# Tiled matmuls in pairs, another order of the first loads, and transposes planned to land later, in an attention and MoE kernel

## The chip, the core and the metric

The kernel runs on one core of one Trainium2 chip. The metric is the device time of one execution in microseconds. Engines are named as in the profile: PE is TensorE (PEld its weight loads), ACT is ScalarE, DVE is VectorE, POOL is GpSimd, SP is SyncE. POOL and SP issue the DMAs here. A time given as "22.5" without more is a moment, counted from the start of the profiled span.

## What is computed

Eight batches of 8 heads, 576 positions and 64 dimensions go through two softmax attentions, and the result through two dense layers with a smooth cut in between:

```python
def sm_attn(qq, kk, vv):
    s = scale * np.matmul(qq, kk.transpose(0, 1, 3, 2))
    a = np.exp(s - np.max(s, axis=-1, keepdims=True))
    a = a / (np.sum(a, axis=-1, keepdims=True) + 1e-09)
    return np.matmul(a, vv)
p_packed = sm_attn(p, k, v)          # p: 32 packed queries per head
out = sm_attn(q, p_packed, p_packed)
x = out.transpose(0, 2, 1, 3).reshape(4608, 512)
h = x @ w_in                         # 512 x 2048
g = np.where(h >= 1, h, np.where(h <= -1, 0.0, (h + 1) ** 2 / 4))
y = g @ w_out                        # 2048 x 512
```

All inputs and the output are float32; the kernel loads with a cast and multiplies in bfloat16.

## The kernel before, in words

The kernel never forms the attention's output. For each batch it works in these steps, whose names are those of the planner's tasks and of the tiles in the profile:

- **kT, qT**: k and q are turned so that the head dimension lies on partitions. For batches 0 to 2 PE does it (`trans`: tile `tp`, L365, then a copy on ACT or DVE); from batch 3 on (`TURNED = 3`) SP issues DMA transposes (`turned`, L489).
- **sc** (L386, tile `sp`): scores of the packed queries against k, then the exponential on ACT (`ex`).
- **pk** (L404, L410): the packed values from `ex` and v, with the sums (`rs`); copies and an addition make `ppT`.
- **s2** (L436, tile `s`): scores of q against the packed values, for one half of the heads (two halves g); ACT takes the exponential (`eT`), PE sums it over 32 rows (`sm`, L446), ACT takes logarithm and exponential (`ln`, `rc`), DVE makes the normalised weights `A`.
- **M** (L478, tile `mp`): packed values times one quarter of w_in, four quarters per batch; a copy on ACT or DVE puts the result into `M`.
- **h** (`hidden_tile`, L521): `M` times `A`, 16 tiles of 128 hidden features per batch, four matmuls each. ACT and DVE apply the smooth cut (`x`, L526 to L533) and write `hT` (L536).
- **o** (`out_tile`, L571): `hT` times w_out. Two batches form a pair of 1152 tokens, that is nine output tiles of 128 rows with 16 matmuls each (one for each of the 16 row blocks of w_out). `ob` is the copy out, and SP issues the writes (L577).

The s2 and M matmuls have 64 rows and 32 columns, so eight of them lie beside each other in PE's array; all others use 128 columns. A task carries the tiling as its `mode`.

The order of the instructions is fixed when the kernel is built. The class `Plan` holds a task for each step with its costs (`C`), dependencies and buffers, simulates the engines DMA, SP, ACT, DVE and PE, and emits each task in the order in which it came up. Three wide PSUM buffers (`"W"`, `NW = 3`) go round among all steps but o, which has two of its own (`"O"`). The DMA engine of the plan takes the loads strictly one after the other, in the order in which they are added; on the chip POOL issues them in that order. `land` is what the plan adds from the end of a load's own cost to its landing, `xt` and `xland` are the same two for a DMA transpose, `p` is when the first part of p is there. While PE has nothing to do in the plan and fewer than three output tiles have begun, it gets dummy matmuls on zeros (L634), which begin at `wake`.

The loads before (L293 to L300) stand in this order: k, v, q of batch 0; w_in and w_out by quarters in turn; k, q, v of batch 1; the rest of p; then k, q, v of batches 2 to 7 as their buffers come free (two buffers for each).

Of the kernel before, what the change touches and what calls it, by code (L numbers as in the profile page):

```python
# [8 lines left out]

C = dict(load=3.0, first=3.8, w_in=2.65, w_out=2.55, out=9.0, p=3.1, land=1.9, xt=5.0, xland=2.5,
         tpp=0.06, tp=0.042, sc=0.034, pk=1.05, s2=0.25, sm=0.245, M=0.345, h=0.49, o=0.217, switch=0.05,
         pTc=0.1, Tca=1.12, Tcd=0.76, ex=0.82, ppT=0.42, ppo=0.41, ppa=0.4, ppd=0.2, rs=0.18, eT=0.74, ln=0.65, rc=0.68, A=0.82,
         Mca=1.0, Mcd=1.22, x=0.65, ta=0.683, td=0.457, hT=0.758, oba=0.585, obd=0.69,
         array=0.2, wake=2.0, tell=0.04, feed=0.1, slack=0.6, margin=0.15, wait=0.5)
NW, NO, NX, NB = 3, 2, 5, 6
DW = 256
TURNED = 3
# [2 lines left out]
class Task:  # L22

    def __init__(self, engines, cost, key, deps, fn, takes, readers, frees, mode, slack, after, holds):
        self.engines, self.cost, self.key, self.deps, self.fn = engines, cost, key, list(deps), fn
        self.takes, self.readers, self.frees, self.mode = takes, readers, frees, mode
        self.slack, self.after, self.holds = slack, after, holds
        self.users, self.end, self.slot, self.gone = [], None, None, 0.0


class Plan:
# [24 lines left out]
    def ready(self, t, e):  # L56
        at = 0.0
        for d in t.deps:
            if e == "PE":
                lag = 0.0 if d.on == "PE" else C["feed"] + (C["margin"] if t.slack is None else t.slack)  # L60
            else:
                lag = C["array"] if d.on == "PE" else C["tell"] if d.on != e else 0.0
            at = max(at, d.end + lag)
        if t.takes:
            room = self.rooms[t.takes][self.count[t.takes] % len(self.rooms[t.takes])]
            if room is None:
                return None
            at = max(at, room + (C["feed"] if e == "PE" else 0.0))
        return at

    def choose(self, e, given, waiting):
# [37 lines left out]
    def run(self, idle):  # L109
        self.line = [t.seq for t in self.tasks if t.engines == ("DMA",)]  # L110
        left = {}
        given = {e: [] for e in self.ENGINES}
        for t in self.tasks:
            left[t] = len(t.deps)
            for d in t.deps:
                d.users.append(t)
            if not t.deps:
                for e in t.engines:
                    given[e].append(t)
        n = len(self.tasks)  # L120
        while n:
            best = None
            for e in self.ENGINES:
                c = self.choose(e, given, n)
                if c is not None and (best is None or c[0] < best[0]):
                    best = c[0], e, c[1]
            if self.count["O"] < 3:
                c, step = self.choose("PE", given, n), DW / 2400
                self.now["PE"] = max(self.now["PE"], C["wake"])
                if (c is None or c[0] > self.now["PE"] + step) and best is not None and best[0] > self.now["PE"]:  # L130
                    idle()
                    self.now["PE"] += step
# [12 lines left out]
            self.log.append((at, at + cost, e, t))  # L145
            if t.takes:
                room = self.rooms[t.takes]
                t.slot = self.count[t.takes] % len(room)
                room[t.slot] = None
                self.count[t.takes] += 1  # L150
                if t.readers == 0:
                    room[t.slot] = t.end + t.holds
            if t.frees is not None:
                f = t.frees
                f.gone = max(f.gone, t.end)
                f.readers -= 1
                if f.readers == 0:
                    self.rooms[f.takes][f.slot] = f.gone
            if len(t.engines) > 1:
                t.fn(e)  # L160
            elif e in ("ACT", "DVE"):
                t.fn(e)
            else:
                t.fn()
            for x in t.engines:
                given[x].remove(t)
            for u in t.users:
                left[u] -= 1
                if left[u] == 0:
                    for x in u.engines:  # L170
                        given[x].append(u)
            n -= 1
# [3 lines left out]
def kernel(  # L176
# [10 lines left out]
    nc = tc.nc  # L187
# [16 lines left out]
    G = 2  # L204
# [8 lines left out]
    NF = d_ff // FW  # L213
# [15 lines left out]
    PE, ACT, DVE, DMA, SP = "PE", "ACT", "DVE", "DMA", "SP"  # L229
# [42 lines left out]
    def add_load(nm, b, parts=1, deps=(), cost="load"):  # L272
        for i, hs in enumerate([ALL] if parts == 1 else HS):
            L[nm, b, i] = add(DMA, C[cost] / parts, -1, deps, lambda nm=nm, b=b, hs=hs: load(nm, b, hs))
        if parts == 1:
            L[nm, b, 1] = L[nm, b, 0]
# [15 lines left out]
    L["v", 0, 0] = L["v", 0, 1] = add(DMA, C["first"], -1, (), lambda: None)  # L292
    add_load("q", 0, 2, cost="first")  # L293
    for f in range(NF):
        add_weights("in", f)
        add_weights("out", f)
    add_load("k", 1)
    add_load("q", 1)
    add_load("v", 1)
    L["p"] = add(DMA, C["load"] / 6, -1, (), lambda: nc.gpsimd.dma_start(p_nat[:, PB * 2:], p_v[:, PB * 2:]))  # L300


    def both(fns, cost_a, cost_d, key, deps, **kw):
# [42 lines left out]
    def attention(b, key):  # L346
# [28 lines left out]
        def scores(i, deps):  # L375
            box, ky = {}, key["sc" + str(i)]

            def mm():
                sp = wide([P, 1024], f32, "sp")
                box["sp"] = sp[:TP, :E * X * Q * NP].rearrange("p (e y) -> p e y", e=E)  # L380
                for e in range(E):
                    o = sp[:, e * X * Q * NP:(e + 1) * X * Q * NP].rearrange("p (x a n) -> p x a n", x=X, a=Q)
                    for a in range(Q):
                        h = head(i, a)
                        w = (h % 4 * E + e) * TP
                        nc.tensor.matmul(o[:, :, a], kT()[:, i, w:w + P], pT[:, b, h], start=True, stop=True)  # L386

            def ev(eng):
                nc.scalar.activation(ex()[:, :, i].rearrange("p e x a n -> p e (x a n)"), box["sp"], AF.Exp, scale=scale)  # L389
            t = add(PE, C["sc"] * 12, ky, deps, mm, takes="W", readers=1, mode=0)  # L390
            return t, add(ACT, C["ex"], ky, [t] + old("pk"), ev, frees=t)

        def packed(deps):
            box, ky = {}, key["pk"]

            def mm():
# [11 lines left out]
                for g in range(G):  # L408
                    for c in range(NC):
                        nc.tensor.matmul(s_[:, g], ex_[:, c // X, g, c % X].rearrange("p a n -> p (a n)"), ones2[:TP],  # L410
                                         start=(c == 0), stop=(c == NC - 1))
            t = add(PE, C["pk"], ky, [L["v", b, 0]] + deps, mm, takes="W", readers=3, mode=0)
            war = old("s2", "M")

            def odd(eng):
# [12 lines left out]
        def weights(g, deps, r):  # L428
# [27 lines left out]
            def norm(eng):  # L456
                nc.vector.scalar_tensor_tensor(A()[:, g], box["eT"], rs()[:, g, :1], box["rc"], ALU.mult, ALU.mult)  # L457
            p_ = K.get((b - 1, "A" + str(g)), [])
            t = add(PE, C["s2"], ky, deps, mm, takes="W", readers=1, mode=2)
            e_ = add(ACT, C["eT"], ky, [t, r] + p_, exp2, frees=t)  # L460
            t2 = add(PE, C["sm"], km, [e_], mm2, takes="W", readers=1, mode=0)
            l_ = add(ACT, C["ln"], km, [t2] + last.get("ln", []), ln, frees=t2)
            i_ = add(ACT, C["rc"], km, [l_] + p_, inv)
            a_ = add(DVE, C["A"], km, [i_] + K.get((b - 2, "h"), []), norm)
            last["ln"] = [i_]
            K[b, "A" + str(g)] = [a_]
            return t, e_, a_

        def mk(f, deps):
            box, ky = {}, key["M" + str(f)]  # L470

            def mm():
                mp = box["mp"] = wide([P, G, FW], f32, "mp")
                for a in range(Q):
                    for g in range(G):
# [1 line left out]
                        y = h % 2  # L477
                        nc.tensor.matmul(mp[a * NP:(a + 1) * NP, g], pp_of(y, h),  # L478
                                         w_in_sb[y * D:(y + 1) * D, h // 2, f * FW:(f + 1) * FW], start=True, stop=True)
            t = add(PE, C["M"], ky, deps + [L["in", f]], mm, takes="W", readers=1, mode=2)  # L480
            cp = lambda eng: copy(M()[:, :, f * FW:(f + 1) * FW], box["mp"])(eng)
            war = K.get((b - 2, "h"), [])
            if (b, f) == (0, 0):
                return t, add(DVE, C["Mcd"], ky, [t], cp, frees=t)
            return t, both(cp, C["Mca"], C["Mcd"], ky, [t] + war, frees=t)

        def turned(nm, i, dst, prev):
            def go():
# [176 lines left out]
```

## Time and profile before

| | |
|---|---|
| median of 3 runs | 257.83 us (256.91 to 258.0) |
| the profiled execution | 256.86 us |
| its span | 255.1 us |
| PE busy in the span | 244.8 us (96%) |
| ACT, DVE busy | 183.9 us, 176.0 us |
| dummy matmuls on PE | 135, 18.3 us |
| loads on POOL's queue | 18.55 MB |

The busy time of PE counts matmuls from start to end, and successive matmuls overlap, so a difference of two starts tells what a group holds of PE better than its duration does. Rows of a timeline give the start, the stretch, the engine, line and operation, out<-in with shapes, the count of instructions merged into the row, and in brackets the idle time before it with what ended it. A row of the waits gives engine, tile and line, what ended the wait, then the sum, the number of times and the longest, in us. A row of DMA issues gives the queue, the size, and the time from the issue to landing.

### The profile page before, as it was taken

To read this page: it belongs to the slowest core of one execution; us is meant where nothing else is said; L and a number is where in the kernel's file an instruction comes from. 1 tells how busy PE (TensorE), PEld (TensorE's weight loads), DVE (VectorE), ACT (ScalarE), POOL (GpSimd) and SP (SyncE) were. 2 spreads that over 40 slices of the span, in tenths; PEclk is the share of its full clock that TensorE was granted. 3 is DMA by queue.
4 is the path that set the end of the run, shared out by engine and by line. 5 is a ranking of instruction groups with operands and counts; after the bars stand their busy time and mean duration, and the time that the engine had idled before them with its cause. 6 is when DMAs were issued, how large, how long until landed. Compare 5 with 4: busy or idle time off the path is not lost.

```text
span 255.1 us, 5583 instructions
## 1 busy us (share of the span) xinstructions
PE 244.8 (96%) x2254; PEld 146.4 (57%) x2287; DVE 176.0 (69%) x303; ACT 183.9 (72%) x295; POOL 28.6 (11%) x41
## 2 busy tenths in 40 slices
PE   7999999899999999999999999999999999999993
PEld 5977557367547555744664556555654465644452
DVE  5236998788899987998847885878366887940000
ACT  3236987888999988989949896989668896841110
POOL 8533312112001300210101000000000000000000
PEclk9999999999999999999999999999999999999998
DMA  7999999999999999999999940211021111132223
GB/s 104 189 207 206 207 204 194 240 210 212 179 200 177 205 182 214 185 193 180 188 150 174 234 116 14 71 44 42 5 80 41 45 41 41 44 82 82 57 70 84
DMA packets 54778, 34.38 MB, mean 135 GB/s; under 512 B 27488, under 2 KB 50272, under 8 KB 54752
## 3 DMA queue, kind: packets, MB, share of 16 engines
q0 software_dynamic: 24624, 18.55, 48.9%
q1 hardware_dynamic: 29968, 15.34, 32.5%
q8 instruction: 18, 0.29, 0.4%
q10 hardware_dynamic: 160, 0.13, 0.2%
q14 instruction: 8, 0.07, 0.1%
HBM read 37.22 MB, written 9.44 MB: 183 GB/s over the span
## 4 chain that ended last, share of the span: by engine, by line
PE 73%; DMA 14%; ACT 3%; DVE 3%; issue 2%; POOL 2%; ACTq 0%; POOLq 0%
PE o L571 42%; PE h L521 22%; DMA p_nat<-in_p_dram 8%; DMA w_out_sb<-in_moe_w_out_dram 7%; PE mp L478 3%; PE sp L386 2%; DVE hT L536 2%; ACT x L526 1%; PE sm L446 1%; PE s L436 1%; ACT x L533 1%; PE tp L365 1%; PE pk L404 1%; POOL w_in_sb L280 1%; POOL q L254 1%
## 5 line engine op out<-in xcount | busy, mean ns | idle before, releaser
L571 PE MATMUL o<-w_out_sb,hT 128*128 128x512 bf16 (+1 forms) x559 | 138.5, 373 | 2.4 <-issue 1.0
L536 DVE SCALAR_TENSOR_TENSOR hT<-x 128x576 bf16<-128x576 f32 x128 | 93.7, 755 | 18.0 <-PE o L571 12.7
L526 ACT ACTIVATE x<-h 128x576 f32<-128x576 f32 x128 | 79.1, 658 | 10.3 <-PE h L521 8.2
L571 PEld LDWEIGHTS <-hT 128*128 128x128 bf16 x592 | 55.9, 98 | 52.4 <-issue 4.8
L521 PE MATMUL h<-A,M 128*128 128x288 bf16 x512 | 79.2, 286 | 1.0 <-ACT M L308 0.3
L521 PEld LDWEIGHTS <-M 128*128 128x128 bf16 x512 | 48.8, 98 | 25.9 <-issue 1.9
L531 DVE TENSOR_SCALAR x<-x 128x576 f32<-128x576 f32 x93 | 42.0, 460 | 16.0 <-ACT x L526 15.4
L308 ACT COPY ob<-o 128x512 f32<-128x512 f32 (+1 forms) x27 | 15.5, 574 | 35.1 <-PE o L571 34.9
L308 ACT CAST M<-mp 128x1024 bf16<-128x1024 f32 x24 | 24.2, 1015 | 0.3 <-PE mp L478 0.3
L308 DVE COPY ob<-o 128x512 f32<-128x512 f32 (+1 forms) x10 | 6.6, 662 | 25.4 <-PE o L571 25.1
L533 ACT ACTIVATE x<-x 128x576 f32<-128x576 f32 x35 | 23.5, 684 | 0.5
L634 PE MATMUL o<-zeros 128*128 128x256 bf16 x135 | 18.3, 286 | 1.2 <-DVE zeros L242 1.2
L389 ACT ACTIVATE ex<-sp 96x768 bf16<-96x768 f32 x16 | 12.9, 804 | 5.0 <-PE sp L386 5.0
L441 ACT ACTIVATE eT<-s,rs 128x576 bf16<-128x576 f32 x16 | 11.9, 746 | 4.8 <-PE s L436 4.8
L634 PEld LDWEIGHTS <-zeros 128*128 128x128 bf16 x135 | 13.1, 102 | 3.7 <-DVE zeros L242 1.2
L457 DVE SCALAR_TENSOR_TENSOR A<-eT,rs,rc 128x576 bf16<-128x576 bf16 x16 | 13.0, 815 | 0.6 <-ACT rc L454 0.6
L478 PE MATMUL mp<-w_in_sb,ppT 64*32 64x512 bf16 x256 | 13.1, 385 | 0.1
L450 ACT ACTIVATE ln<-sm 128x576 f32<-128x576 f32 x16 | 10.5, 656 | 2.9 <-PE sm L446 2.8
L254 POOL DMA_DIRECT2D q<-in_q_dram x9 | 7.3, 815 | 46.1 <-DMA qT<-q 34.6
L254 POOL DMA_DIRECT2D k<-in_k_dram x9 | 6.9, 767 | 40.0 <-DMA kT<-k 19.3
L454 ACT ACTIVATE rc<-ln 128x576 f32<-128x576 f32 x16 | 10.9, 682 | 0.5
L308 DVE CAST M<-mp 128x1024 bf16<-128x1024 f32 x8 | 9.8, 1220 | 1.6 <-PE mp L478 1.5
(46 smaller groups left out, 115.2 us busy)
## 6 DMA issues: line engine op xcount, KB each, us to landing
v<-in_v_dram POOLq DMA_DIRECT2D x8, 576.0 KB, 15.5
out_dram<-ob SPq DMA_DIRECT2D x23, 192.0 KB, 2.5
k<-in_k_dram POOLq DMA_DIRECT2D x7, 576.0 KB, 16.6
q<-in_q_dram POOLq DMA_DIRECT2D x7, 576.0 KB, 12.6
out_dram<-ob SPq DMA_DIRECT2D x24, 128.0 KB, 2.4
w_in_sb<-in_moe_w_in_dram POOLq DMA_DIRECT2D x4, 512.0 KB, 16.9
w_out_sb<-in_moe_w_out_dram POOLq DMA_DIRECT2D x4, 512.0 KB, 17.6
out_dram<-ob SPq DMA_DIRECT2D x23, 64.0 KB, 2.1
```

The source lines that it names most:

```text
L254: nc.gpsimd.dma_start(tok[nm, b][:, hs].rearrange("p h c d -> p h (c d)"), SRC[nm][b, hs].rearrange("h (p c) d -> p h (c d)", c=NC))
L308: return lambda eng: nc.vector.tensor_copy(out_, in_) if eng == DVE else nc.scalar.copy(out_, in_)
L389: nc.scalar.activation(ex()[:, :, i].rearrange("p e x a n -> p e (x a n)"), box["sp"], AF.Exp, scale=scale)
L457: nc.vector.scalar_tensor_tensor(A()[:, g], box["eT"], rs()[:, g, :1], box["rc"], ALU.mult, ALU.mult)
L478: nc.tensor.matmul(mp[a * NP:(a + 1) * NP, g], pp_of(y, h), w_in_sb[y * D:(y + 1) * D, h // 2, f * FW:(f + 1) * FW], start=True, stop=True)
L521: nc.tensor.matmul(h[:, hf, :HALF], T[b, "M"][:, g, fi * P:(fi + 1) * P], T[b, "A"][:, g, hf], start=(g == 0), stop=(g == G - 1))
L526: nc.scalar.activation(box["x"], box["h"][:, :, :HALF], AF.Prelu, bias=-1.0, alpha=0.5)
L531: nc.vector.tensor_scalar(x, x, 1.0, 0.0, ALU.add, ALU.max)
L533: nc.scalar.activation(x, x, AF.Relu, bias=1.0)
L536: nc.vector.scalar_tensor_tensor(hT[:, fi, col:col + S].rearrange("p (a t) -> p a t", a=2), box["x"], 1.0, box["x"], ALU.min, ALU.mult)
L571: nc.tensor.matmul(o, hT[:, fi, i * P:(i + 1) * P], w_out_sb[:, fi, cs], start=(fi == 0), stop=(fi == KF - 1))
L634: plan.run(lambda: nc.tensor.matmul(o[:, :DW], zeros[:, :P], zeros[:, :DW], start=True, stop=True))
```

## The change

The pairs: in `attention`, s2 and M become generators that hand their matmuls to a new `tiled`, which makes one PE task of one or two of them. From batch 2 on the pairs are (s2 of half 0, M of quarter 0), (s2 of half 1, M of quarter 1) and (M of quarters 2 and 3). A task can therefore claim several buffers, and the planner's bookkeeping of `readers`, `slots` and `frees` becomes lists. `join` is what the plan deducts for the second of a pair. s2 and M get dependencies on tasks of earlier batches up front, on PE.

The loads: w_in's second quarter goes ahead of w_out's first, and so on; batch 1's k and q come in two halves, v goes ahead of q, and all three ahead of the last quarter of w_out. Costs of loads, `p`, `land` and `wake` are set anew. `xland` goes from 2.5 to 11.0, so that the plan puts the users of a DMA transpose later.

```diff
-C = dict(load=3.0, first=3.8, w_in=2.65, w_out=2.55, out=9.0, p=3.1, land=1.9, xt=5.0, xland=2.5,
-         tpp=0.06, tp=0.042, sc=0.034, pk=1.05, s2=0.25, sm=0.245, M=0.345, h=0.49, o=0.217, switch=0.05,
+C = dict(load=2.95, v0=3.6, q0=2.76, w_in=2.57, w_out=2.57, rest=1.25, out=9.0, p=4.05, land=1.75, xt=5.0, xland=11.0,
+         tpp=0.06, tp=0.042, sc=0.034, pk=1.05, s2=0.25, sm=0.245, M=0.345, h=0.49, o=0.217, switch=0.05, join=0.15,
...
-         array=0.2, wake=2.0, tell=0.04, feed=0.1, slack=0.6, margin=0.15, wait=0.5)
+         array=0.2, wake=1.2, tell=0.04, feed=0.1, slack=0.6, margin=0.15, wait=0.5)
...
-            room = self.rooms[t.takes][self.count[t.takes] % len(self.rooms[t.takes])]
-            if room is None:
-                return None
-            at = max(at, room + (C["feed"] if e == "PE" else 0.0))
+            rooms = self.rooms[t.takes]
+            for j in range(len(t.readers)):
+                room = rooms[(self.count[t.takes] + j) % len(rooms)]
+                if room is None:
+                    return None
+                at = max(at, room + (C["feed"] if e == "PE" else 0.0))
...
-    add_load("q", 0, 2, cost="first")
-    for f in range(NF):
-        add_weights("in", f)
-        add_weights("out", f)
-    add_load("k", 1)
-    add_load("q", 1)
-    add_load("v", 1)
+    add_load("q", 0, 2, cost="q0")
+    add_weights("in", 0)
+    add_weights("in", 1)
+    add_weights("out", 0)
+    add_weights("in", 2)
+    add_weights("out", 1)
+    add_weights("in", 3)
+    add_weights("out", 2)
+    add_load("k", 1, 2)
+    add_load("v", 1, 1)
+    add_load("q", 1, 2)
+    add_weights("out", 3)
...
-            t = add(PE, C["sc"] * 12, ky, deps, mm, takes="W", readers=1, mode=0)
+            t = add(PE, C["sc"] * 12, ky, deps + old("pk"), mm, takes="W", readers=1, mode=0)
...
-            t = add(PE, C["pk"], ky, [L["v", b, 0]] + deps, mm, takes="W", readers=3, mode=0)
+            t = add(PE, C["pk"], ky, [L["v", b, 0]] + deps + old("s2", "M", "A"), mm, takes="W", readers=3, mode=0)
...
-            t = add(PE, C["s2"], ky, deps, mm, takes="W", readers=1, mode=2)
-            e_ = add(ACT, C["eT"], ky, [t, r] + p_, exp2, frees=t)
+            t, j = yield ky, C["s2"], deps + p_, mm
+            e_ = add(ACT, C["eT"], ky, [t, r] + p_, exp2, frees=(t, j))
...
-            t = add(PE, C["M"], ky, deps + [L["in", f]], mm, takes="W", readers=1, mode=2)
+            t, j = yield ky, C["M"], deps + [L["in", f]] + K.get((b - 2, "h"), []), mm
...
+        def tiled(*units):
+
+            units = list(units)
+            asked = [next(u) for u in units]
+            t = add(PE, sum(a[1] for a in asked) - C["join"] * (len(asked) - 1), asked[0][0], [d for a in asked for d in a[2]],
+                    lambda: [a[3]() for a in asked], takes="W", readers=[1] * len(units), mode=2)
+            return [u.send((t, j)) for j, u in enumerate(units)]
...
-        ws = [weights(g, pc + (qc0, qc1)[g], r) for g in range(G)]
-        ms = [mk(f, pc) for f in range(NF)]
+        ws, ms = [weights(g, pc + (qc0, qc1)[g], r) for g in range(G)], [mk(f, pc) for f in range(NF)]
+        if b < 2:
+            ws, ms = [tiled(w)[0] for w in ws], [tiled(m)[0] for m in ms]
+        else:
+            pairs = [tiled(w, m) for w, m in zip(ws, ms)] + [tiled(*ms[2:])]
+            ws, ms = [p_[0] for p_ in pairs[:2]], [p_[1] for p_ in pairs[:2]] + pairs[2]
```

More of the change, by code (lines that the diff above doesn't have):

```diff
@@ L25, in __init__ @@
         self.engines, self.cost, self.key, self.deps, self.fn = engines, cost, key, list(deps), fn
-        self.takes, self.readers, self.frees, self.mode = takes, readers, frees, mode
-        self.slack, self.after, self.holds = slack, after, holds
-        self.users, self.end, self.slot, self.gone = [], None, None, 0.0
+        self.takes, self.readers = takes, list(readers) if isinstance(readers, (list, tuple)) else [readers]
+        self.frees = (frees, 0) if isinstance(frees, Task) else frees
+        self.mode, self.slack, self.after, self.holds = mode, slack, after, holds
+        self.users, self.end, self.slots, self.gone = [], None, None, [0.0] * len(self.readers)
 class Plan:
@@ L147, in run @@
                 room = self.rooms[t.takes]
[L148 to L152, printed above, removed]
-            if t.frees is not None:
[L154 to L158, printed above, removed]
+                t.slots = [(self.count[t.takes] + j) % len(room) for j in range(len(t.readers))]
+                self.count[t.takes] += len(t.slots)
+                for n_, j in zip(t.readers, t.slots):
+                    room[j] = None if n_ else t.end + t.holds
+            if t.frees is not None:
+                f, j = t.frees
+                f.gone[j] = max(f.gone[j], t.end)
+                f.readers[j] -= 1
+                if f.readers[j] == 0:
+                    self.rooms[f.takes][f.slots[j]] = f.gone[j]
             if len(t.engines) > 1:
@@ L291 @@
     L["k", 0, 1] = add(DMA, C["load"] / 2, -1, (), lambda: None)
-    L["v", 0, 0] = L["v", 0, 1] = add(DMA, C["first"], -1, (), lambda: None)
-    add_load("q", 0, 2, cost="first")
-    for f in range(NF):
-        add_weights("in", f)
-        add_weights("out", f)
-    add_load("k", 1)
-    add_load("q", 1)
-    add_load("v", 1)
-    L["p"] = add(DMA, C["load"] / 6, -1, (), lambda: nc.gpsimd.dma_start(p_nat[:, PB * 2:], p_v[:, PB * 2:]))
+    L["v", 0, 0] = L["v", 0, 1] = add(DMA, C["v0"], -1, (), lambda: None)
+    add_load("q", 0, 2, cost="q0")
[10 more added lines that the diff above has]
+    add_weights("out", 3)
+    L["p"] = add(DMA, C["rest"], -1, (), lambda: nc.gpsimd.dma_start(p_nat[:, PB * 2:], p_v[:, PB * 2:]))
     def both(fns, cost_a, cost_d, key, deps, **kw):
@@ L466, in weights @@
             K[b, "A" + str(g)] = [a_]
-            return t, e_, a_
+            yield t, e_, a_
         def mk(f, deps):
@@ L483, in mk @@
             if (b, f) == (0, 0):
-                return t, add(DVE, C["Mcd"], ky, [t], cp, frees=t)
-            return t, both(cp, C["Mca"], C["Mcd"], ky, [t] + war, frees=t)
+                yield t, add(DVE, C["Mcd"], ky, [t], cp, frees=(t, j))
+            yield t, both(cp, C["Mca"], C["Mcd"], ky, [t] + war, frees=(t, j))
+        def tiled(*units):
[4 more added lines that the diff above has]
+            return [u.send((t, j)) for j, u in enumerate(units)]
         def turned(nm, i, dst, prev):
```

## The prediction

> **What bounds the kernel now.** I read the shares of busy time first, then PE's waits, then PE's timeline.
>
> ```profile
> span 255.1 us, 5583 instructions
> PE 244.8 (96%) x2254; PEld 146.4 (57%) x2287; DVE 176.0 (69%) x303; ACT 183.9 (72%) x295; POOL 28.6 (11%) x41
> ```
> ```profile
> PE o L571 <- issue: 1.0, 6, 0.2
> ...
> PE s L436 <- ACT eT L441: 0.4, 1, 0.4
> PE h L521 <- ACT M L308: 0.3, 1, 0.3
> PE o L571 <- DVE hT L536: 0.3, 1, 0.3
> PE o L571 <- ACT ob L308: 0.2, 1, 0.2
> ```
>
> PE is busy for 244.8 of 255.1 us; its waits behind the first work are 1.2 us on ACT and DVE (last four lines) and 1.0 us of "issue". So there is one bound, PE's fixed order, and the span is what PE does plus where it stands still. Two kinds of its time can still shrink: dummy matmuls at the start, and the drains at each change of tiling. The start:
>
> ```profile
> 1.20 2.74 PE L634 MATMUL o<-zeros 128*128 128x256 bf16 x12 [1.20 <-DVE zeros L242]
> ...
> 4.46 3.22 PE L634 MATMUL o<-zeros 128*128 128x256 bf16 x28
> 7.52 0.68 PE L365 MATMUL tp<-ident,k 96*128 96x96 bf16 x12
> ...
> 12.63 0.86 PE L404 MATMUL pk<-ex,v 96*128 96x64 bf16 x24
> ...
> 19.66 0.41 PE L446 MATMUL sm<-eT,onesblk 128*128 128x288 bf16 x2
> ...
> 22.52 1.63 PE L521 MATMUL h<-A,M 128*128 128x288 bf16 x12
> ```
> ```profile
> 20.85 0.68 ACT L454 ACTIVATE rc<-ln 128x576 f32<-128x576 f32 x1
> ```
> ```profile
> 21.56 0.82 DVE L457 SCALAR_TENSOR_TENSOR A<-eT,rs,rc 128x576 bf16<-128x576 bf16 x1 [0.15 <-ACT rc L454]
> ```
>
> Until 22.52 PE is mostly filler: the first hidden tile waits for the chain sm (19.66), two logarithms and exponentials on ACT, A on DVE (to 22.38). From 22.52 on nearly everything is real work. The profiled execution took 256.86 us, 1.76 over its span; the median of the runs is 257.83, 0.97 above it.
>
> **The change, part by part.** PE's order of the two kernels gives the counts: 135 dummies become 124.
>
> *Start.* The dummies now begin at the planner's 1.2 instead of 2.0 and p is taken for later (4.05 for 3.1), so 29 stand ahead of the transpose of p. The first 12 took 2.74 us (about 0.21 each), the 28 behind 4.46 took 3.06 to the next start (0.11 each): 14 or 15 slow ones from 1.20, the rest fast, end near 5.9; transpose of p, 17 dummies, first transpose of k at 7.9 (before 7.52, k had landed by then). That 0.4 us is won back in the shorter filler behind it: pk at 12.8 with 13 fillers for 15, three for seven ahead of q's first transpose, eight for eleven ahead of the second. The second s then goes out at about 17.2 instead of 18.19, its exponential ends at 18.35, sm follows at 18.5 for 19.66; ACT needs four passes of 0.65 to 0.68 from 18.35 (21.0), A ends at 21.9, first hidden tile at 22.0. Gain 0.5 us; bounds 0 (the chain is as long as before) and 1.1 (sm's whole advance).
>
> In the filled places stands also the second M (mp, w_in's second quarter, which now lands ahead of w_out), a group of 0.44 us (below) that stood behind the first hidden tile: gain 0.43. Of dummies, 7 stood behind that tile, now 3: 4 x 0.11 = 0.43. M and hidden tiles can use their weights sooner, so the 0.33 wait for M goes.
>
> *Pairs.* What a group in the 64x32 tiling costs:
>
> ```profile
> 65.29 0.32 PE L436 MATMUL s<-qT,ppT 64*32 64x288 bf16 x8
> 65.42 0.40 PE L478 MATMUL mp<-w_in_sb,ppT 64*32 64x512 bf16 x8
> 65.75 0.39 PE L571 MATMUL o<-w_out_sb,hT 128*128 128x512 bf16 x1
> ...
> 66.78 0.32 PE L436 MATMUL s<-qT,ppT 64*32 64x288 bf16 x8
> 67.03 0.61 PE L571 MATMUL o<-w_out_sb,hT 128*128 128x512 bf16 x2
> ...
> 73.84 0.66 PE L521 MATMUL h<-A,M 128*128 128x288 bf16 x4
> 74.43 0.41 PE L478 MATMUL mp<-w_in_sb,ppT 64*32 64x512 bf16 x8
> 74.77 0.61 PE L571 MATMUL o<-w_out_sb,hT 128*128 128x512 bf16 x2
> ```
>
> Alone, s holds PE 0.25 (66.78 to 67.03), mp 0.34 (74.43 to 74.77). Ahead of mp lies a gap: four h at 0.122 (1.63 for 12 against 0.66 for 4, so 8 in 0.97) end at 74.33, mp starts 0.10 later. With it they cost 0.35 and 0.44, together 0.79. Side by side s and mp take 0.46 (65.29 to 65.75) plus one gap, 0.56: a merge saves 0.22. By PE's order batches 2 to 7 had 31 such groups (this s with mp already adjacent in five batches), now three each, 18: 13 merges, 2.9 us. Six of these join mp with mp, which the trace never shows: the second then costs between 0.22 (as it streams behind s, scaled from 0.13 by 512/288) and 0.34 (no overlap), a saving of 0.22 to 0.10. I take the former, the nearer row in kind; the bound is 2.1 us for all. The five "issue" waits of 0.16 behind the close pair of M's in batches 2 to 7 (0.8) have no place left. Batch 1 puts its s, mp, s side by side: another 0.1. A pair claims two of the three wide PSUM buffers at once; where that delays the next hidden tile is a rival below.
>
> *Loads.* When they land, issue plus time to landing:
>
> ```profile
> 5.42 0.76 POOL L280 DMA_DIRECT2D w_in_sb<-in_moe_w_in_dram  x1
> ...
> 14.24 0.74 POOL L282 DMA_DIRECT2D w_out_sb<-in_moe_w_out_dram  x1 [0.64 <-DMA q<-in_q_dram]
> ...
> 22.12 0.77 POOL L254 DMA_DIRECT2D v<-in_v_dram  x1 [1.74 <-DMA w_in_sb<-in_moe_w_in_dram]
> ```
> ```profile
> w_in_sb<-in_moe_w_in_dram POOLq DMA_DIRECT2D x1, 512.0 KB, 11.3
> ```
> ```profile
> w_out_sb<-in_moe_w_out_dram POOLq DMA_DIRECT2D x1, 512.0 KB, 20.6
> ```
> ```profile
> v<-in_v_dram POOLq DMA_DIRECT2D x1, 576.0 KB, 21.4
> ```
>
> First w_in 16.72, last w_out 34.84: seven quarters behind the first, 2.59 each. Batch 1's k, q, v follow till 43.52: 2.89 each. With six quarters ahead, k now lands at 35.1, v at 38.0, q's first half at 39.5, its second at 40.9, and the last w_out at 43.5 instead of 34.8. POOL issues two more loads (halves, 0.77 each) and had waits to spare.
>
> The price: from 22.0 PE has, ahead of q's first transpose, 64 h (7.8), 24 o, 3 dummies (0.3), two mp (0.9), two transposes of k (0.5 each) and two sp (0.35). One o is 0.216:
>
> ```profile
> 93.76 2.97 PE L571 MATMUL o<-w_out_sb,hT 128*128 128x512 bf16 x13
> 96.57 0.65 PE L521 MATMUL h<-A,M 128*128 128x288 bf16 x4
> ```
>
> so 5.2; in all 15.9, done at 37.9. Without the last w_out only 12 of 16 steps of two output tiles can run, and those are the 24: nothing else is in reach, PE stands until 39.5. Loss 1.6. Then batch 1's chain. Before, from pk to its first hidden tile:
>
> ```profile
> 43.58 0.86 PE L404 MATMUL pk<-ex,v 96*128 96x64 bf16 x24
> ...
> 52.79 0.65 PE L521 MATMUL h<-A,M 128*128 128x288 bf16 x4
> ```
>
> 9.21 us. Now pk at 40.0 (behind q's transpose) gives 49.2. PE's own work from 39.5 till there is 8.2 (15 o, six 64x32 units in four groups, two sm, pk, transposes): ready at 47.7, so 1.5 more is lost, 3.1 together. Bounds: 1.6 (the chain hidden) and 4.6 (it is 1.5 longer). Batch 1 still starts 3.6 us sooner than before, but PE has stood still for most of that.
>
> The other edits (readers as lists, dependencies on tasks two batches back) issue nothing: their cost is nothing but the order counted above.
>
> *Transposes.* The planned landing only moves their users:
>
> ```profile
> 62.29 6.14 SPq L489 DMA_TRANSPOSE kT<-k  x1
> ```
> ```profile
> kT<-k SPq DMA_TRANSPOSE x1, 16.3
> ```
> ```profile
> 80.16 0.51 PE L386 MATMUL sp<-pT,kT 128*128 128x64 bf16 x12
> ```
>
> Batch 3's second half of k landed at 78.6, its use came at 80.16. Now PE reaches that use 29.2 us of work behind 49.2, at 78.4. On SP the same output writes stand ahead of it. I take no loss: later batches have more distance. Bounds 0 and the first rival's.
>
> *Sum:* 0.5 + 0.43 + 0.43 + 2.9 + 0.1 + 0.8 + 1.2 (the four old waits) - 3.1 = 3.3. Span 251.8, that execution 253.6, median 254.6 (0.97 on top).
>
> **Rivals.** *Late transposes (the slower side).* The loads of batch 4 are let go some 4 us sooner and share the engines with batch 3's transposes. DMA is full there:
>
> ```profile
> 53.00:78.00 25.00, 24.27 (x262) 15.09 (x266) 22.20 (x37) 22.55 (x37) 2.33 (x3) 1.00 1.30 198
> 251.00:255.10 4.10, 0.00 (x0) 0.00 (x0) 0.16 (x1) 0.00 (x0) 0.00 (x0) 0.80 0.23 66
> ```
>
> (the second last figure is the DMA share, 1.30 with overlapping packets, the one ahead of it the granted clock). If one 576 KB load overtakes, the transpose lands 2.9 later, at 81.5, and 3.1 us are lost at that sp: 257.7, no change. If two do, 84.4, a loss of 6.0: 260.6. It decides from a landing at 82.8 on. Against it: SP can issue it earlier too. The Trainium skill (DMA: Bandwidth & Descriptors, "Queues, rings and completion order") says that a DMA engine goes round robin between the queues that have work; that speaks for this rival, and the landing of 16.3 beside three loads agrees.
>
> *Evictions take the pairs' gain.* In that window DVE and ACT are busy 22.2 and 22.55 of 25 us. If holding two buffers turns the 2.9 into waits for ACT and DVE, the median is 257.5, no change. Against it: the hidden tiles of batches 1 to 7 get as long as before, with the same work: the last 153 output matmuls, behind which no hidden tile is left in either order, began here
>
> ```profile
> 221.13 10.74 PE o L571 x49
> ```
>
> 168.3 us behind 52.79, and by the sum (221.13 - 3.3) begin 168.6 behind 49.2.
>
> *The clock falls in the gap.* The last row has a mean granted clock of 0.80 after PE stopped, so it drops within such a pause. Between 37.9 and 45 PE works about half. Falling back would cost one warm-up, as from 1.20 to 4.46, at half speed: 1.6 us, 256.2. Against it: no single pause comes to more than 1.6. The Trainium skill (TensorE: Matmul & The Clock Gate, "Why this matters for your kernels") asks for no idle gap over about 3 us; by that rule this does not happen.
>
> **How the numbers follow.** Chances: forecast 0.69, late transposes 0.12 (two loads 0.09, one 0.03), evictions 0.12, clock 0.07. The predicted time is the forecast's, 254.6. Its own range is 252.8 (only the first 1.6 of the two waits, and 0.3 more at the start) to 256.4 (merges 2.1, no start gain, a little more in batch 1). The whole range takes in the clock and the evictions: 252.8 to 257.6. A change below 0.5%, 1.3 us, is about what a measurement can't tell: faster (under 256.5) is forecast and clock, 0.76; same 0.15; slower 0.09.
>
> **What would show it.** First h near 22.0; PE idle 1 to 2 us ahead of q's first transpose, ended by the load of q, and again up to a first h of batch 1 near 49; 16 mp in one row of about 0.56 us to the next start; no issue waits; sp of batch 3 unhindered. It is wrong if PE waits for kT, or for ACT and DVE behind pairs, by more than 2 us, or if batch 1's chain takes much longer than 9.2.

## The result, and the profile after

The changed kernel takes 253.77 us (median of 4 runs, 253.03 to 254.32), the kernel before 257.6: a ratio of 0.9862, 95% interval 0.9839 to 0.9886, so 1.4% faster. The forecast was 254.6, with 252.8 to 257.6 around it. The profiled execution took 253.44 us with a span of 251.7, and the sum had come to a span of 251.8. The total is right, but not all of its terms are: it has too much for the start and for the waits on "issue" and too little for the loads, and these errors nearly cancel. That part of the agreement is luck, as the experiments and the traces show.

The page of the changed kernel, its busy shares, and PE's waits (engine, tile and line, what ended the wait, sum, times, longest):

```profile
span 251.7 us, 5563 instructions
PE 242.1 (96%) x2244; PEld 146.0 (58%) x2276; DVE 181.0 (72%) x306; ACT 181.9 (72%) x292; POOL 28.8 (11%) x43
```
```profile
PE s L444 <- DVE ppT L427: 0.4, 1, 0.4
PE sm L454 <- ACT eT L449: 0.3, 1, 0.3
PE tp L373 <- DMA q<-in_q_dram: 0.3, 1, 0.3
PE o L591 <- issue: 0.3, 2, 0.2
PE h L541 <- ACT x L546: 0.3, 2, 0.2
PE h L541 <- ACT kT L316: 0.3, 1, 0.3
PE sm L454 <- issue: 0.2, 1, 0.2
```

PE is still the bound, at 96%. The first three waits are new and stand in batch 1's chain. None is for a DMA transpose: the `kT` in the last but one line is ACT's copy for batch 2, at 53.26. PE's timeline at the places that the prediction named:

```profile
1.19 5.47 PE L654 MATMUL o<-zeros 128*128 128x256 bf16 x29 [1.19 <-DVE zeros L245]
6.50 0.28 PE L328 MATMUL tpp<-ident,p_nat 128*128 128x128 bf16 x2
...
8.47 0.67 PE L373 MATMUL tp<-ident,k 96*128 96x96 bf16 x12
...
22.50 2.12 PE L541 MATMUL h<-A,M 128*128 128x288 bf16 x16
...
39.66 0.68 PE L373 MATMUL tp<-ident,q 96*128 96x96 bf16 x12 [0.34 <-DMA q<-in_q_dram]
40.17 0.86 PE L412 MATMUL pk<-ex,v 96*128 96x64 bf16 x24
...
49.35 0.66 PE L541 MATMUL h<-A,M 128*128 128x288 bf16 x4
...
75.12 0.63 PE L486 MATMUL mp<-w_in_sb,ppT 64*32 64x512 bf16 x16
75.68 0.67 PE L541 MATMUL h<-A,M 128*128 128x288 bf16 x4
...
79.27 0.51 PE L394 MATMUL sp<-pT,kT 128*128 128x64 bf16 x12
```
```profile
217.58 0.59 PE L591 MATMUL o<-w_out_sb,hT 128*128 128x512 bf16 x2
```

The first hidden tile starts at 22.50, where it was 22.52 before: nothing was won at the start. Batch 1's first hidden tile starts at 49.35 for 52.79, the last 153 output matmuls at 217.58 for 221.13. From 49.35 to there it is 168.2 us, as many as before (168.3), though 11 more output matmuls lie in it, which before had come ahead of batch 1's first hidden tile (39 for 50 by PE's order): the saving of the pairs shows as more work in the same stretch. Two M side by side (75.12 to 75.68) hold PE for 0.56.

### The profile page after: what moved, and what is told of

The parts are those of the page before. It is cut to its first block, busy times and chain, and to the rows that moved or that the text cites. A ratio compares the mean times of both kernels' runs of the same rounds, so it can differ in the third digit from the quotient of the medians.

```text
span 251.7 us, 5563 instructions
## 1 busy us (share of the span) xinstructions
PE 242.1 (96%) x2244; PEld 146.0 (58%) x2276; DVE 181.0 (72%) x306; ACT 181.9 (72%) x292; POOL 28.8 (11%) x43
## 4 chain that ended last, share of the span: by engine, by line
PE 76%; DMA 13%; DVE 3%; ACT 3%; POOL 2%; issue 2%; DVEq 0%; ACTq 0%; POOLq 0%
PE o L591 43%; PE h L541 22%; DMA q<-in_q_dram 7%; DMA w_out_sb<-in_moe_w_out_dram 6%; PE mp L486 3%; PE pk L412 2%; PE sp L394 2%; PE s L444 1%; DVE hT L556 1%; PE sm L454 1%; PE tp L373 1%; PE pk L418 1%; DVE ob L316 1%; POOL w_in_sb L283 1%; ACT rc L462 1%
## 5 line engine op out<-in xcount | busy, mean ns | idle before, releaser
L591 PE MATMUL o<-w_out_sb,hT 128*128 128x512 bf16 (+1 forms) x560 | 135.2, 373 | 1.2 <-issue 0.3
L591 PEld LDWEIGHTS <-hT 128*128 128x128 bf16 x592 | 56.5, 98 | 53.7 <-issue 3.8
L546 ACT ACTIVATE x<-h 128x576 f32<-128x576 f32 x128 | 77.4, 652 | 9.6 <-PE h L541 5.1
L541 PE MATMUL h<-A,M 128*128 128x288 bf16 x512 | 76.9, 286 | 1.1 <-ACT x L546 0.3
L551 DVE TENSOR_SCALAR x<-x 128x576 f32<-128x576 f32 x84 | 38.4, 458 | 6.2 <-ACT x L546 5.0
L316 ACT COPY ob<-o 128x512 f32<-128x512 f32 (+1 forms) x24 | 13.8, 576 | 31.9 <-PE o L591 30.3
L553 ACT ACTIVATE x<-x 128x576 f32<-128x576 f32 x44 | 29.8, 683 | 0.5
L316 DVE COPY ob<-o 128x512 f32<-128x512 f32 (+1 forms) x13 | 8.7, 667 | 26.6 <-PE o L591 26.1
L316 DVE CAST M<-mp 128x1024 bf16<-128x1024 f32 x15 | 18.3, 1220 | 2.9 <-PE mp L486 2.8
L316 ACT CAST M<-mp 128x1024 bf16<-128x1024 f32 x17 | 16.9, 1006 | 1.0 <-PE mp L486 1.0
L486 PE MATMUL mp<-w_in_sb,ppT 64*32 64x512 bf16 x256 | 11.9, 381 | 0.3
## 6 DMA issues: line engine op xcount, KB each, us to landing
v<-in_v_dram POOLq DMA_DIRECT2D x8, 576.0 KB, 15.9
w_out_sb<-in_moe_w_out_dram POOLq DMA_DIRECT2D x4, 512.0 KB, 17.5
```

Source lines behind the costliest of these rows:

```text
L316: return lambda eng: nc.vector.tensor_copy(out_, in_) if eng == DVE else nc.scalar.copy(out_, in_)
L486: nc.tensor.matmul(mp[a * NP:(a + 1) * NP, g], pp_of(y, h), w_in_sb[y * D:(y + 1) * D, h // 2, f * FW:(f + 1) * FW], start=True, stop=True)
L541: nc.tensor.matmul(h[:, hf, :HALF], T[b, "M"][:, g, fi * P:(fi + 1) * P], T[b, "A"][:, g, hf], start=(g == 0), stop=(g == G - 1))
L546: nc.scalar.activation(box["x"], box["h"][:, :, :HALF], AF.Prelu, bias=-1.0, alpha=0.5)
L551: nc.vector.tensor_scalar(x, x, 1.0, 0.0, ALU.add, ALU.max)
L553: nc.scalar.activation(x, x, AF.Relu, bias=1.0)
```

## The experiments

Each kernel was timed against the kernel before on the same chip; that one's median was 257.2 to 257.5 us there. The diffs are against the changed kernel; where one goes back to the kernel before in several places, the loads are the lines of the diff in the second experiment.

**The pairs undone.**

```diff
-        if b < 2:
+        if b < B:
             ws, ms = [tiled(w)[0] for w in ws], [tiled(m)[0] for m in ms]
```

> The changed kernel with s2 and M of batches 2 to 7 as single tasks again; loads, start and landing as changed. PE's order then has 41 groups in the 64x32 tiling for 28. Theory (the pairs are worth their drains on PE, and PE is the bound): 13 x 0.22 = 2.9 us and some issue waits more, median 256.6 to 257.2 where the changed kernel has 253.8. Rival (ACT and DVE take the pairs' gain): within 0.6 us of the changed kernel.

Measured: 256.44 us, 2.7 more than the changed kernel and a little under the theory's range. In the profiles batch 1's first hidden tile is at nearly the same place (49.01 for 49.35), and from there to the end it takes 205.2 us for 202.3: 2.9, which is 13 merges at 0.22. ACT and DVE took nothing of it. But this kernel has no wait on "issue" in its list either, so the vanished issue waits were no effect of the pairs. They were no waits at all. The profile of this kernel has a record for every matmul, as many as weight loads; that of the kernel before has 33 fewer (2254 for 2287), and where it shows "issue", a record is missing. First the page of the kernel without pairs, then two rows of the kernel before:

```profile
PE 247.3 (97%) x2276; PEld 146.3 (58%) x2276; DVE 176.5 (69%) x304; ACT 184.2 (72%) x294; POOL 29.3 (12%) x43
```
```profile
50.31 0.33 PEld L571 LDWEIGHTS <-hT 128*128 128x128 bf16 x3 [0.23 <-issue]
50.54 0.59 PE L571 MATMUL o<-w_out_sb,hT 128*128 128x512 bf16 x2 [0.16 <-issue]
```

There are three weight loads and two matmuls: the output matmul that belongs between 50.31 and 50.54 is not in the trace. Of the 14 profiles the eleven without missing records list no "issue" wait of PE; the three that list some lack 32 to 34 records each, nearly all of output matmuls.

**The pairs alone**, with the loads, costs, start and landing of before.

```diff
-C = dict(load=2.95, v0=3.6, q0=2.76, w_in=2.57, w_out=2.57, rest=1.25, out=9.0, p=4.05, land=1.75, xt=5.0, xland=11.0,
+C = dict(load=3.0, v0=3.8, q0=3.8, w_in=2.65, w_out=2.55, rest=0.5, out=9.0, p=3.1, land=1.9, xt=5.0, xland=2.5,
...
-         array=0.2, wake=1.2, tell=0.04, feed=0.1, slack=0.6, margin=0.15, wait=0.5)
+         array=0.2, wake=2.0, tell=0.04, feed=0.1, slack=0.6, margin=0.15, wait=0.5)
...
-    add_weights("in", 0)
-    add_weights("in", 1)
...
-    add_weights("out", 3)
+    for f in range(NF):
+        add_weights("in", f)
+        add_weights("out", f)
+    add_load("k", 1)
+    add_load("q", 1)
+    add_load("v", 1)
```

> The pairs alone, with the loads, costs, landing and start of the kernel before (29 groups for 42, 135 dummies). Theory (by the prediction's sum the pairs with their issue waits are 3.8 us and all that was done to loads and start comes to about nothing): 253.5 to 254.4, as the changed kernel. Rival (the order of the loads brings a good part): 255 to 256.5.

Measured: 263.87 us, 6.6 us slower than the kernel before. Neither theory nor rival had this. PE's timeline of this kernel:

```profile
70.17 0.52 PE L389 MATMUL sp<-pT,kT 128*128 128x64 bf16 x12 [0.22 <-DMA kT<-k]
70.53 0.38 PE L586 MATMUL o<-w_out_sb,hT 128*128 128x512 bf16 x1
77.38 0.82 PE L389 MATMUL sp<-pT,kT 128*128 128x64 bf16 x12 [6.46 <-DMA kT<-k]
78.01 3.51 PE L586 MATMUL o<-w_out_sb,hT 128*128 128x512 bf16 x8
```

With pairs the plan orders batch 3's two `sp` right behind each other, and the second half of `kT` is not there for 6.46 us. Behind it 8 output matmuls take 3.51 us, twice their usual time: the clock fell in the wait.

**The landing undone alone.**

```diff
-C = dict(... xt=5.0, xland=11.0,
+C = dict(... xt=5.0, xland=2.5,
```

> The changed kernel with xland back at 2.5 alone. Theory (with pairs the plan moves the users of the DMA transposes; only the late landing keeps them behind the real one): both sp of batch 3 stand right behind each other in PE's order, reached near 70, the second half of k lands near 77 to 79, PE waits 6 to 8 us there, its clock falls in that wait, and the median is 260 to 264. Rival (the landing does nothing, as the prediction has it): 253.4 to 254.2.

Measured: 261.73 us, 8 more than the changed kernel, as the theory had it. The wait and the busy times around it (the granted clock is the third figure from the end):

```profile
77.77 0.82 PE L394 MATMUL sp<-pT,kT 128*128 128x64 bf16 x12 [6.78 <-DMA kT<-k]
```
```profile
70.60:74.60 4.00, 0.39 (x7) 0.08 (x3) 1.94 (x4) 1.20 (x2) 0.00 (x0) 1.00 1.27 191
74.60:81.40 6.80, 3.63 (x33) 1.37 (x33) 0.00 (x0) 1.04 (x2) 1.54 (x2) 0.50 1.18 218
```

6.8 us are the wait, the rest is work at half clock up to 81.4. The transposes do not land later than in other runs (the half that is waited for arrives at 77.7, in the changed kernel at 78.4); it is PE's order that comes for them too soon.

**The landing alone, on the kernel before**: no pairs; loads, costs and start as before.

```diff
-        if b < 2:
+        if b < B:
...
-C = dict(load=2.95, v0=3.6, q0=2.76, w_in=2.57, w_out=2.57, rest=1.25, out=9.0, p=4.05, land=1.75, xt=5.0, xland=11.0,
+C = dict(load=3.0, v0=3.8, q0=3.8, w_in=2.65, w_out=2.55, rest=0.5, out=9.0, p=3.1, land=1.9, xt=5.0, xland=11.0,
...
-         wake=1.2
+         wake=2.0
```

> The kernel before with xland at 11.0 alone: no pairs, loads, costs and start as before. Theory (before had no wait for a transpose, so there is nothing to win): within 0.6 us of the kernel before. Rival (the later landing itself is a gain): faster by over 1.3 us.

Measured: 257.5 us against 257.53, ratio 0.9999 (0.998 to 1.0017). The later landing has no gain of its own.

**Pairs and landing**, with loads, costs and start as before: the kernel just shown, with its first two lines left as

```diff
         if b < 2:
```

> The kernel before with pairs and xland at 11.0; loads, costs and start as before. Theory (the pairs are worth 2.7 us once no transpose is waited for, whatever the loads do): 254.2 to 254.9. Rival (with the old order of the loads the pairs' gain is lost in batch 1's chain, as in the run with the old loads): 256 to 256.6.

Measured: 255.04 us, ratio 0.9917 (0.989 to 0.9944), just above the theory's range: 2.5 us faster than the kernel with the landing alone. That is the pairs' worth once more. The changed kernel is 1.3 us faster still; the order and costs of the loads are all that is left to bring this, as the start does nothing (two runs below).

**The loads in the order of before**, the rest as changed.

```diff
-    add_weights("in", 0)
-    add_weights("in", 1)
...
-    add_weights("out", 3)
+    for f in range(NF):
+        add_weights("in", f)
+        add_weights("out", f)
+    add_load("k", 1)
+    add_load("q", 1)
+    add_load("v", 1)
```

> The changed kernel with the loads in the order of before (w_in and w_out in turn, then k, q, v of batch 1 whole); pairs, costs, start and landing as changed. Theory: the first hidden tile and batch 1 come later, but PE has 11 more output matmuls within reach in between, so the median is within 0.8 us of the changed kernel. Rival (the load order is needed for the gain): 255 or more.

Measured: 256.21 us, 2.4 more than the changed kernel, as the rival had it. Here PE waits 0.7 for k, 0.5 for q, 0.5 for pk and 1.3 for `eT`, and batch 1's first hidden tile comes at 55.49. It is also 1.2 slower than pairs and landing with all of the old costs, so the new costs of load and start, which fit the new order, make a worse plan around the old one, and the 2.4 is not the worth of the order alone. What the plan did differently there was not tried apart.

**The start of before** in the changed kernel.

```diff
-p=4.05, land=1.75
+p=3.1, land=1.9
...
-wake=1.2
+wake=2.0
```

> The changed kernel with p, land and wake of before: 12 dummies ahead of the transpose of p for 29, six fewer in all before k's first transpose. Theory (batch 1's chain hangs on the landing of q's first half near 39.6): first hidden tile 0.6 to 0.9 us sooner, the wait ahead of q's first transpose longer by as much (about 1.0 for 0.34), median within 0.4 us of the changed kernel. Rival (the start counts one for one): 252.9 to 253.2.

Measured: 253.93 us, the theory's median. The first hidden tile starts at 22.12 (for 22.50), q's first transpose at 39.27, batch 1's first hidden tile at 49.36: the same to 0.01. The 0.4 was not given back where the theory had it, though. In this run q's first half landed 0.4 sooner (39.2 for 39.6), so the wait for it stayed at 0.33; PE lost the time behind it, 0.26 to q's second half and 0.39 to the copy of `qT`.

**17 dummies fewer**; PE's order is otherwise the same.

```diff
-wake=1.2
+wake=3.0
```

> The changed kernel with wake at 3.0: 12 dummies ahead of the transpose of p for 29, nothing else in PE's order differs. Theory (batch 1's chain hangs on q's first half, near 39.6): the first hidden tile comes 1 to 2 us sooner, PE waits for loads by as much longer further on, and the median is within 0.4 us of the changed kernel. Rival (a shorter start counts one for one): 251.8 to 252.8.

Measured: 253.74 us, within the theory's 0.4. The first hidden tile starts 1.15 us sooner, at 21.35, and PE gives it back:

```profile
PE tp L373 <- DMA q<-in_q_dram: 0.9, 1, 0.9
PE sp L394 <- DMA kT<-k: 0.8, 1, 0.8
...
PE tp L373 <- DMA k<-in_k_dram: 0.2, 1, 0.2
```

The wait of 0.8 for `kT` is the prediction's first rival in small, but not at batch 3. There the second half of k landed at 77.0, ahead of its use; the wait stands two batches later:

```profile
78.98 0.51 PE L394 MATMUL sp<-pT,kT 128*128 128x64 bf16 x12
...
120.80 0.52 PE L394 MATMUL sp<-pT,kT 128*128 128x64 bf16 x12 [0.81 <-DMA kT<-k]
```

Batch 5's second half was issued at 103.7 here and in the changed kernel, and landed at 120.7 here and at 119.7 there, 0.45 ahead of its use at 120.11. That is the tightest place of the planned landing.

**The last quarter of w_out ahead of batch 1's loads.**

```diff
     add_weights("out", 2)
+    add_weights("out", 3)
     add_load("k", 1, 2)
     add_load("v", 1, 1)
     add_load("q", 1, 2)
-    add_weights("out", 3)
```

> The changed kernel with the last quarter of w_out ahead of batch 1's k, v and q. Theory (PE stands still ahead of q's transpose because w_out is late, and 18 output matmuls come within reach ahead of batch 1's first hidden tile, 3.9 us, while that tile comes 2.6 us later with q): 1.3 us faster than the changed kernel, 252.3 to 252.9. Rival (the chain of batch 1 sets the end, what is filled in between is not won): 1.5 us or more slower, 255 to 256.5.

Measured: 256.45 us, 2.7 slower than the changed kernel, as the rival had it. q's first transpose starts at 41.89, pk at 42.41, the first hidden tile of batch 1 only at 54.53. That is 12.1 us behind pk and not 9.2: with output matmuls within reach the plan spreads the chain out, and the second `s` waits 1.4 for ACT.

**Batch 1's q ahead of its v**, the one swap undone.

```diff
     add_load("k", 1, 2)
-    add_load("v", 1, 1)
     add_load("q", 1, 2)
+    add_load("v", 1, 1)
```

> The changed kernel with batch 1's q ahead of its v. Theory (the chain from pk to the first hidden tile is 9.2 us and then hangs on v, which lands near 41.0 instead of 38): first hidden tile of batch 1 near 50.2 for 49.35, median 254.2 to 254.8. Rival (with q already turned the chain behind pk is shorter by the second transpose): 253.3 to 253.8.

Measured: 253.62 us (252.73 to 254.58); the median is the rival's. In the profile, taken of the longest of its four runs, v lands at 41.0 and pk starts later, at 41.06 for 40.17, as the theory had it. Batch 1's first hidden tile comes at 51.42, later than the theory's 50.2, because the clock falls behind a single wait of 1.22 us:

```profile
43.43 0.57 PE L444 MATMUL s<-qT,ppT 64*32 64x288 bf16 x8 [1.22 <-DVE ppT L427]
...
45.36 1.06 PE L591 MATMUL o<-w_out_sb,hT 128*128 128x512 bf16 x2
```
```profile
41.10:44.50 3.40, 2.18 (x63) 1.48 (x63) 2.68 (x8) 1.59 (x4) 0.77 (x1) 1.00 1.71 185
44.50:47.90 3.40, 3.40 (x24) 0.94 (x22) 2.42 (x3) 2.27 (x4) 0.00 (x0) 0.50 1.31 204
```

Half speed for 3.4 us costs up to 1.7. The four runs lie at 252.73, 252.8, 254.44 and 254.58, 1.7 apart in two groups, which would fit a clock that falls in every second run. The mean granted clock of each run says the same: 0.999 and 0.997 in the two shorter ones, 0.992 and 0.993 in the two longer. So q ahead of v was 1.0 us below the changed kernel's median where the clock stayed up, and 0.7 to 0.8 above it where it fell; two runs of each are too few to say how often it falls. Why it falls here is open: in the kernel with w_out ahead PE was busy for less of an equal stretch, with a wait of 1.41 in it, and the clock stayed up.

```profile
46.60:50.00 3.40, 1.97 (x24) 0.92 (x24) 2.52 (x3) 2.51 (x4) 0.00 (x0) 1.00 1.26 238
```

**pk ahead of q's transposes** in batch 1's keys.

```diff
     for b in range(1, B):
         lo, hi = (b - 1 + 0.05, b - 0.05)
+        now = order if b > 1 else "kT0 kT1 sc0 sc1 pk qT0 qT1 s20 M0 s21 sm0 M1 sm1 M2 M3".split()
-        keys[b] = {nm: lo + (hi - lo) * i / len(order) for i, nm in enumerate(order)}
+        keys[b] = {nm: lo + (hi - lo) * i / len(order) for i, nm in enumerate(now)}
```

> The changed kernel with batch 1's pk ahead of the transposes of its q in the plan's keys, so that PE does not wait for q's first half ahead of pk. Theory (the wait for q delays the chain): pk near 39.3 for 40.17, first hidden tile of batch 1 0.5 to 0.9 us sooner, median 252.9 to 253.4. Rival (q's second half, near 41, holds s and the chain anyway): within 0.4 us of the changed kernel.

Measured: 252.95 us, ratio to the kernel before 0.9827 (0.9804 to 0.985), the lowest median of all, 0.8 under the changed kernel (the intervals overlap a little). pk starts at 39.17 and the wait for q is gone. Batch 1's first hidden tile did not come sooner, though: 49.76, since `s` now waits 0.5 for the copy of `qT` and an M 0.6 for a buffer. The gain is that PE does more ahead of it: one more output matmul, and batch 2's first transpose, and two groups of the small tiling fewer (26 for 28 in all). The theory had the time right and the way wrong.

**Batch 1's loads ahead of the last two quarters of w_out**, with pk first and the start of before.

```diff
-    add_weights("out", 2)
     add_load("k", 1, 2)
     add_load("v", 1, 1)
     add_load("q", 1, 2)
+    add_weights("out", 2)
     add_weights("out", 3)
```

> The changed kernel with batch 1's k, v, q ahead of the last two quarters of w_out, pk ahead of the transposes of q in batch 1's keys, and p, land and wake of before. Theory (what is left to win lies in PE's gap around batch 1's chain): q's first half lands near 37 for 39.6, hidden tiles of batch 0 stand in the gap, PE waits less than 0.5 us there, median 251.8 to 252.6. Rival (the sooner PE is, the longer it waits for batch 3's DMA transposes): a wait of 1 us or more for kT near 75, 252.8 to 253.6.

Measured: 254.16 us, above the ranges of both theory and rival. pk starts at 37.78, no wait for a transpose shows, and PE now waits for DVE: near 35 and 36, where DVE still had batch 0's hidden tiles to do, and at 51, for its copy of the transposed p:

```profile
PE h L541 <- DVE pT L316: 1.0, 1, 1.0
PE h L541 <- DVE M L316: 0.7, 1, 0.7
PE sp L394 <- DVE kT L316: 0.7, 1, 0.7
```

## Why the prediction was right, and where it was not

**PE's fixed order is the bound, and idle PE is the account.** Right: every gain and loss above is found in PE's waits or in PE's groups.

**The pairs at 2.9 us.** Right: 2.9 in the profiles and 2.7 in the medians by undoing them, 2.5 by adding them to the landing. Two M side by side cost what the nearer row had said, 0.56 with no sign of the upper bound. The 0.8 for issue waits was wrong: PE never stood still there. In each of these places an output matmul has its weight load but no record of its own in the profile before (first experiment), and the 0.3 and 0.2 that are left in the profile after are of the same kind.

**The start at 0.5.** Wrong between these two profiles: 0.02. The step took PE's clock to rise at the same moment as in the profile before. The busy times of both, before first:

```profile
4.40:5.50 1.10, 1.10 (x12) 0.99 (x13) 0.28 (x1) 0.49 (x2) 1.10 (x3) 1.00 1.28 193
```
```profile
4.40:5.50 1.10, 1.10 (x7) 0.79 (x6) 0.00 (x0) 0.00 (x0) 1.10 (x3) 1.00 1.26 187
```

In the same stretch PE ran 12 matmuls before, at 0.11 or less each, and 7 after: still half speed, so the 29 dummies ended at 6.5 and not at 5.9. (The column of the granted clock reads 1.00 in both rows; the trace's record of the clock begins only with the rise, at 4.3 before and at 5.6 after.) The moment moves from run to run whatever the kernel: in the kernel with the landing alone, whose start is that of before, there are 7 in this stretch too, and its first hidden tile comes at 23.74. Where the clock rises at about the same moment in both, the step comes out: with the start of before 23.74 (rise at 6.88) and 23.41 (the pairs alone, 6.20), with the new one 23.18 (q ahead of v, 6.98) and 22.85 (the landing undone, 6.31), 0.56 sooner each time. The profile of before had an early one, and thereby a lower time than its median. That is also why 0.97 between profile and median was too much to carry over (0.33 after).

**The start does not count.** The prediction had the reason, the landing of q's first half (forecast 39.5; PE started on it at 39.66), but priced the start as if its 0.5 were kept, and then let the wait ahead of q take 1.6. They are one sum: start earlier, wait longer. The runs with six and with 17 dummies fewer show it: 0.4 and 1.15 us won at the first hidden tile are 0 and 0.3 at that of batch 1. PE came to q's transpose at 39.3 and not 37.9, 0.5 of it by the later start and the rest through small gaps that the sum left out, so the wait was 0.34.

**Batch 1's chain of 9.2.** Right: 40.17 to 49.35 is 9.18.

**The loads as a whole.** This is the step that failed: it is wrong in sign. The sum had them, with the start and the old waits, at 0.5 us lost (0.5 + 0.43 + 0.43 + 1.2 - 3.1); the changed kernel is 1.3 us faster than pairs and landing alone. The term behind it is the 3.1, the time for which PE stands still ahead of batch 1's first hidden tile. The rows from the first hidden tile of batch 0 to that of batch 1, with the loads of before (the landing alone) and with the new ones (the pairs undone); both profiles have a record for every matmul, and up to there PE does the same work as in the kernels before and after:

```profile
23.74:53.68 29.94, 28.80 (x326) 17.07 (x324) 25.05 (x41) 25.21 (x39) 5.93 (x7) 1.00 1.33 210
```
```profile
22.67:49.01 26.34, 25.22 (x290) 15.08 (x288) 22.91 (x37) 23.42 (x38) 7.15 (x9) 1.00 1.34 202
```

With the new loads PE is idle for 1.12 us of the stretch (26.34 less 25.22), where the sum had 3.1; with those of before it is idle for 1.14, where the sum counted waits of 0.9. So the loads cost PE about nothing there, and not some 2 us. Ahead of q's first transpose the sum had 15.9 us of work and the profile of the changed kernel has 16.5, which fills most of the wait of 1.6; in the chain behind it PE is idle there for 1.0 and not 1.5. The clock has a part too: the profile before had an early rise, and in the three kernels with its loads and costs and a rise at 6.2 to 6.9 batch 1's first hidden tile comes at 53.5 to 53.7 and not 52.79, while the five with the new loads and chain have it at 49.0 to 49.4 (rises at 5.5 to 6.4). How much of the 1.8 us between the sum and the measurement is clock and how much idle time was not tried apart.

**The transposes' landing "only moves their users".** Wrong as a price. On the kernel before it is worth nothing, as forecast; with pairs it is worth 8 us, because the plan otherwise brings both `sp` of batch 3 to 70, where k's second half is 7 us away. The mechanism was known (78.6 against 80.16 in the profile before), but the step never asked what the pairs would do to the order without it. Its remark that later batches have more distance was wrong as well: batch 5 has 0.45 in the changed kernel where batch 3 has 0.9.

**The rivals.** Late transposes did not happen in the changed kernel (`sp` at 79.27, the landing at 78.4, 0.9 apart) and did, for 0.8 us at batch 5, in the kernel with 17 dummies fewer. Evictions took nothing. The clock did not fall; it fell in the profiles of three variants, and one of them had no wait over 1.22 us. The prediction leaned on the Trainium skill (TensorE: Matmul & The Clock Gate, "Why this matters for your kernels"), which asks for no idle gap over about 3 us, and took shorter pauses for safe; the measurement shows one that was not. The Trainium skill (the same page, "A second HAM failure mode: psum-queue depth-cycling") also tells of a kernel whose clock goes back and forth because PE idles briefly and often between groups of matmuls. That run has one pause and one fall, PE busy 2.18 of 3.40 us and then 0.50 clock for as long, so it is no instance of this.

## What to carry to other kernels

In a kernel whose order is fixed by a plan, an assumption in the plan can be worth nothing until another change makes the plan lean on it, as the landing was here: test pairs of edits, and not each edit alone. Where the chain hangs on a landing, time won ahead of it is given back at it, and only work that can be moved across the landing counts. Small groups in another array tiling are worth merging: the 13 merges saved 0.22 us each on average here, drain and overlap together. And before idle time on PE is priced, count the matmul records against the weight loads: an "issue" wait can be a matmul without a record.

## What was not expected of the hardware

The clock's rise at the start came anywhere between 3.9 and 7.0 us behind the span's start in the 14 profiles, though PE began at 1.19 to 1.20 in all of them. In a wait of 6.5 to 6.8 us the clock fell some 3.6 us behind the end of the last matmul and stayed at half for 6.8 us, the last 3.6 to 3.9 us of it dense work. A DMA transpose of k landed between 4.3 and 17.5 us behind its issue in the changed kernel, with the same shape each time; the one of batch 5 that is the tightest took 15.9 there and 17.0 in the kernel with 17 dummies fewer, issued at the same moment.
